# Moving one chunk's scaling to VectorE and its transposes to TensorE in the first stage of a fused attention and feed-forward kernel

## Chip, cores, metric

One core of a Trainium2 chip. The metric is the device time of one execution in microseconds (us). A profile's *span* is some 1.8 us shorter than the time of the same execution, because it starts with the first recorded instruction. "Fast" runs are those at the normal granted clock.

## The reference, cut to what matters

```python
def rmsnorm(x, g):                       # q, k: (8, 12, 448, 64), per head
    rms = np.sqrt(np.mean(x * x, axis=-1, keepdims=True) + 1e-06)
    return x / rms * g
scores = scale * np.matmul(q_n, k_n.transpose(0, 1, 3, 2))
attn = ...                               # softmax of the scores (cut)
x = np.matmul(attn, v)                   # -> (3584, 768)
h = x @ w_in                             # 768 -> 2048
g = h + np.sin(alpha * h) ** 2 / (alpha + 1e-09)
out = g @ w_out                          # 2048 -> 768
```

## The kernel before

It works by batch. Batch b has an *attention stage* (three chunks of four heads; scores, exponentials, values) and a *first product* (h and the sine). The second product of batch b-1 fills TensorE's gaps in the attention stage of batch b. So the first attention stage (b = 0) has no filler but dummy products ("warm"), and the second (b = 1) is the first to be interleaved. Before a chunk's scores it needs square, reduce, rsqrt, scale, and a transposition of q and k. The first three chunks ("early") do the scaling on VectorE and the transposition on TensorE. All later chunks use GpSimd and DMA:

```python
early = ci < NC                                     # NC = 3 chunks a batch
def scale(w):
    eng = nc.vector if early else nc.gpsimd         # inv in PSUM if early, in SBUF if not
def transpose():                                    # DMA
    nc.sync.dma_start_transpose(out=qkT[pi]..., in_=st.n[...])
def pe_transpose(pairs, ws=(0, 1), act=False):      # 28 transposes into one PSUM pair, then copies
    tp = bank_pair("tp", BF16)
```

PSUM is handed out as four pairs of banks. The allocator takes the pair that its own model expects to be free first, and the instruction then waits for the pair's last reader:

```python
def bank_pair(name, dtype=F32):
    slot = min(free_at, key=free_at.get)
    ...
def values(n=1):                                    # the last two value pairs of a batch: n = 2
    if n == 1:
        return attend(pairs.popleft())
    for js in (range(NJ - 1), [NJ - 1]):            # six tiles of one pair, six of the other,
        for pi in list(pairs)[:n]:                  # then the last tile of each
            attend(pi, js)
```

The end of the first stage (S_ is one tile of scores with its warm products, A_ a value pair; cut):

```python
A_(), S_(1), S_(1), S_(1)
c2.pe_transpose((0, 1))
S_(2), A_(), S_(2)
step_of(NC, 3, 4)()                # fourth chunk (NC): reduce
S_(2), S_(1), A_()
step_of(NC, 5, 6)()                # rsqrt, scale on GpSimd, DMA transpose
load_w_out(1)
S_(1), S_(1), A_(), S_()
step_of(NC + 1, 3, 4)()            # fifth chunk: reduce
S_(), A_(2)
```

## Time and profile before

| | before |
|---|---|
| time, median of 3 | 439.43 us |
| span of the profiled execution | 438.3 us (time 440.08 us) |
| first attention stage | 0 to 39.56 us, TensorE idle 5.95 us |
| first product | 39.56 to 57.73 us, no idle |
| second attention stage | 57.73 to 92.72 us, TensorE idle 4.11 us |
| all after it | 345.58 us, idle only in the last output's drain |

A row of the timeline reads: start, length, engine, source line, operation, output<-inputs, shape, count, and in brackets the engine's idle time ahead of it and what ended that. Source lines named here: L294 scores, L297 exponentials, L314 values, L320 and L321 reciprocals, L326 normalization of the values, L246 scaling, L269 TensorE transposes, L276 copies of the transposed tile, L353 first product, L400 second product, L406 output copies.

One view is needed that the prediction does not show: TensorE in the last two value pairs of the first stage.

```profile
35.88 0.38 PE L314 MATMUL av<-expT,vb 64*64 64x448 bf16 x2 [0.23 <-ACT expT L297]
...
37.73 0.38 PE L314 MATMUL av<-expT,vb 64*64 64x448 bf16 x2 [0.71 <-ACT expT L297]
```

Five tiles of the first pair run from 35.88, then TensorE waits 0.71 us for the sixth tile's exponential.

### The profile page before, as it was taken

Reading aid. Unit: us, or ns where it says so; the run is one execution under the profiler, and the core shown is the slowest. Engines: PE = TensorE matmul, PEld = TensorE weight load, DVE = VectorE, ACT = ScalarE, POOL = GpSimd, SP = SyncE. Lnnn points to the kernel's source line nnn. Section 1 sums busy time; section 2 is a strip of 40 time slices with the busy share of each in tenths; the row PEclk is TensorE's granted clock in tenths of the full one; section 3 lists DMA queues with packets and bytes.
Section 4 is the critical chain, followed back from the end, with each engine's and each line's share of the span. In section 5 each row is a group of like instructions: output and inputs, shape, how many; then the busy total and the mean of one; then the engine's idle time right before and its main releaser. Section 6 shows DMA issues by size and latency. Waiting matters only on the chain.

```text
span 438.3 us, 9452 instructions
## 1 busy us (share of the span) xinstructions
PE 423.9 (97%) x3817; PEld 220.3 (50%) x3819; DVE 227.5 (52%) x329; ACT 340.0 (78%) x532; POOL 280.5 (64%) x264
## 2 busy tenths in 40 slices
PE   7889988999999999999999999999999999999996
PEld 3434543555555555555555554555555555555563
DVE  4767463547454574455636574555635474246511
ACT  5888897878888788878888788887878788788600
POOL 4969869917797469937699269956599276003300
PEclk9999999999999999999999999999999999999999
DMA  7999999790067804593076903596063901320022
GB/s 252 210 255 189 188 214 243 226 231 6 20 181 194 176 2 94 152 211 114 2 199 167 204 0 50 167 214 141 2 179 100 125 0 28 90 56 0 1 72 73
DMA packets 70096, 55.09 MB, mean 126 GB/s; under 512 B 41492, under 2 KB 65828, under 8 KB 70052
## 3 DMA queue, kind: packets, MB, share of 16 engines
q1 hardware_dynamic: 56690, 40.97, 36.9%
q0 software_dynamic: 12416, 11.81, 18.0%
q10 hardware_dynamic: 946, 1.70, 1.0%
q8 instruction: 30, 0.49, 0.4%
q14 instruction: 14, 0.11, 0.1%
HBM read 45.62 MB, written 11.01 MB: 129 GB/s over the span
## 4 chain that ended last, share of the span: by engine, by line
PE 83%; ACT 4%; DMA 4%; POOL 4%; DVE 2%; issue 2%; POOLq 0%; ACTq 0%
PE ops L400 31%; PE hps L353 30%; PE av L314 13%; PE sc L294 8%; DMA qkT<-qkn 3%; POOL qk L224 2%; ACT expT L297 2%; ACT s L332 1%; DMA qk<-in_k_dram 1%; POOL sq L221 1%; DVE ms L227 1%; DVE xT L326 1%; ACT s L337 1%; POOL vb L135 1%; DVE qkn L246 0%
## 5 line engine op out<-in xcount | busy, mean ns | idle before, releaser
L297 ACT ACTIVATE expT<-sc 128x896 bf16<-128x896 f32 x168 | 144.5, 912 | 31.9 <-PE sc L294 31.2
L400 PE MATMUL ops<-w_out_sb,g_sb 128*128 128x384 bf16 x896 | 156.7, 327 | 0.0
L353 PE MATMUL hps<-xT,w_in 128*128 128x448 bf16 x768 | 146.7, 353 | 0.0
L335 POOL TENSOR_TENSOR s<-s 128x448 f32<-128x448 f32 x61 | 56.7, 934 | 114.6 <-ACT s L332 100.4
L400 PEld LDWEIGHTS <-g_sb 128*128 128x128 bf16 x896 | 83.1, 98 | 69.5 <-issue 18.4
L340 DVE SCALAR_TENSOR_TENSOR g_sb<-s,inv_alpha_sb,hps 128x448 bf16<-128x448 f32 x128 | 80.8, 676 | 63.3 <-POOL s L335 62.3
L353 PEld LDWEIGHTS <-w_in 128*128 128x128 bf16 x768 | 74.5, 98 | 71.5 <-issue 2.9
L326 DVE TENSOR_TENSOR xT<-av,rec 64x448 bf16<-64x448 f32 x96 | 59.7, 622 | 70.6 <-ACT rec L321 51.5
L332 ACT ACTIVATE s<-hps,alpha_sb 128x448 f32<-128x448 f32 x128 | 74.9, 627 | 26.7 <-PE hps L353 23.9
L246 POOL TENSOR_TENSOR qkn<-qk,inv 128x448 bf16<-128x448 f32 x84 | 76.2, 940 | 10.0 <-POOL qk L224 6.0
L221 POOL TENSOR_TENSOR sq<-qk 128x896 f32<-128x896 f32 x44 | 73.4, 1686 | 0.0
L314 PE MATMUL av<-expT,vb 64*64 64x448 bf16 x672 | 69.2, 349 | 1.8 <-ACT expT L297 0.9
L314 PE MATMUL av<-expT,ones 64*64 64x448 bf16 x672 | 69.2, 349 | 0.0
L294 PE MATMUL sc<-qkT 64*64 64x448 bf16 x672 | 51.8, 361 | 4.4 <-DMA qkT<-qkn 1.8
L227 DVE TENSOR_REDUCE ms<-sq 128x14 f32<-128x896 f32 x44 | 46.8, 1081 | 16.3 <-POOL sq L221 16.1
L406 DVE COPY osb<-ops 128x768 f32<-128x768 f32 (+1 forms) x33 | 27.6, 837 | 46.7 <-PE ops L400 40.1
L224 POOL TENSOR_TENSOR qk<-qk,gg 128x896 f32<-128x896 f32 x24 | 50.2, 2091 | 1.8 <-ACT gg L171 1.7
L314 PEld LDWEIGHTS <-vb 64*64 64x64 bf16 x672 | 37.6, 107 | 14.0 <-issue 2.6
L314 PEld LDWEIGHTS <-ones 64*64 64x64 bf16 x672 | 37.1, 107 | 11.6
L337 ACT ACTIVATE s<-s 128x448 f32<-128x448 f32 x67 | 38.6, 577 | 3.5 <-DVE g_sb L340 0.5
L294 PEld LDWEIGHTS <-qkT 64*64 64x64 bf16 x672 | 15.3, 104 | 34.4 <-issue 28.5
L320 ACT ACTIVATE rec<-av 128x448 f32<-128x448 f32 x48 | 26.1, 544 | 3.7 <-PE av L314 3.2
(44 smaller groups left out, 136.6 us busy)
## 6 DMA issues: line engine op xcount, KB each, us to landing
qk<-in_q_dram SPq DMA_DIRECT2D x24, 448.0 KB, 5.5
qk<-in_k_dram SPq DMA_DIRECT2D x22, 448.0 KB, 5.9
out_dram<-osb SPq DMA_DIRECT2D x39, 192.0 KB, 2.8
vb<-in_v_dram POOLq DMA_DIRECT2D x32, 168.0 KB, 6.6
w_in<-in_moe_w_in_dram POOLq DMA_DIRECT2D x4, 768.0 KB, 11.0
w_out_sb<-in_moe_w_out_dram POOLq DMA_DIRECT2D x2, 1536.0 KB, 25.2
out_dram<-osb SPq DMA_DIRECT2D x26, 96.0 KB, 6.2
qk<-in_k_dram ACTq DMA_DIRECT2D x2, 448.0 KB, 6.0
```

The source lines that it names most:

```text
L221: nc.gpsimd.tensor_mul(st.sq[w], qk[ci][:, w], qk[ci][:, w])
L224: eng.tensor_mul(qk[ci][:, 0], qk[ci][:, 0], gg.to_broadcast([P, 2 * NJ, D]))
L246: eng.tensor_mul(n[:, :, hi, :], x[:, hi], inv[:, hi].unsqueeze(2).to_broadcast([P, NJ, D]))
L294: nc.tensor.matmul(sc[key_rows(pp, hi), pp, :S], qkt[r, 1, j * REST:(j + 1) * REST], qkt[r, 0, :], start=True, stop=True)
L297: nc.scalar.activation(expT[c, j], sc[:, :, :S], ACT.Exp, scale=SCALE)
L314: nc.tensor.matmul(av[o, part, :S], ones[r, :] if part else vb[b][r, hp, j, :], expT[pi // 2, j][r, pi % 2, :], start=(j == 0), stop=(j == ...
L326: nc.vector.tensor_mul(xT[b][r, hp, :], av[r, 0, :S], rec[o, :])
L332: nc.scalar.activation(s1, hps, ACT.Sin, scale=alpha_sb[:, m, :])
L335: nc.gpsimd.tensor_mul(s2, s1, s1)
L340: nc.vector.scalar_tensor_tensor(g_sb[:, m, (b % 2) * S:(b % 2 + 1) * S], s2, inv_alpha_sb[:, m, :], hps, op0=ALU.mult, op1=ALU.add)
L353: nc.tensor.matmul(ps[:, m % 2, :S], w_in_sb[m * 2 // MT][:, kt, m % (MT // 2) * P:(m % (MT // 2) + 1) * P], x[:, kt, :], start=(kt == 0), ...
L400: nc.tensor.matmul(st["ps"][:, k, :HALF], g_sb[:, m, c0:c0 + P], w_out_sb[:, m, half * HALF:(half + 1) * HALF], start=(m == 0), stop=(m == ...
```

## The change

The intent: take the fourth chunk off GpSimd and the DMA queues, which are both behind when the second stage begins, and put it into the first stage, where TensorE runs dummies. With it come several smaller edits. The core of the diff:

```diff
-        give_back(ps, passes(0.2) + 0.5)          # alpha
+        give_back(ps, passes(0.2) + 2.0)
-        early = ci < NC
+        early = ci <= NC
-        def scale(w):
+        def scale(w, heads=(0, 1)):               # may now be cut by heads
-        if m % 2 == 0 and (b or m <= MT // 2):    # squares on GpSimd
+        if m % 2 == 0:
-            for js in (range(NJ - 1), [NJ - 1]):
+            for j in range(NJ):
                 for pi in list(pairs)[:n]:
-                    attend(pi, js)
+                    attend(pi, [j])
@@ first stage
+    spread_alpha()                                # moved here, ahead of the third rsqrt
     c2.rsqrt()
     ...
+    load_w_out(1)                                 # moved ahead
+    c4.fold_g()                                   # moved ahead
     A_(), S_(1), S_(1), S_(1)
     c2.pe_transpose((0, 1))
-    S_(2), A_(), S_(2)
-    step_of(NC, 3, 4)()
-    S_(2), S_(1), A_()
-    step_of(NC, 5, 6)()
-    load_w_out(1)
-    S_(1), S_(1), A_(), S_()
+    S_()
+    c3.reduce(0), c3.reduce(1)
+    A_(), S_(2)
+    c3.rsqrt()
+    S_(2)
+    c3.scale(0), c3.scale(1)
+    load_qk(NC + 3)
+    S_(1), A_(), S_(1), S_(1)
+    c3.pe_transpose((0, 1))
+    A_(), S_()
@@ beside the first product (i: after the i-th pair of tiles)
-    (2, c4.fold_g), (4, c4.scale(0)), (5, c4.scale(1)), (6, transpose)
+    (2, c4.scale(0, [0])), (3, c4.scale(0, [1])), (4, c4.scale(1, [0])), (5, c4.scale(1, [1])),
+    (6, transpose), (6, the sixth chunk's second square)
```

More of the change, by code (lines that the diff above doesn't have):

```diff
@@ L244, in scale @@
             inv = st.inv[w].rearrange("p (hi j) -> p hi j", hi=2)
-            for hi in range(2):
+            for hi in heads:
                 eng.tensor_mul(n[:, :, hi, :], x[:, hi], inv[:, hi].unsqueeze(2).to_broadcast([P, NJ, D]))
-            st.scaled += 1
-            if st.scaled == 2:
+            st.scaled += len(heads)
+            if st.scaled == 4:
                 for ps, time in st.inv_ps:
@@ L452 @@
     c0.pe_transpose((0, 1), (0,))
-    spread_alpha()
     c1.reduce(0), c1.reduce(1)
@@ L499 @@
     begin_norm(NC)
-    step_of(NC, 0, 1, 2)()
+    c3 = norm[NC]
+    c3.square(0), c3.square(1)
+    c3.fold_g()
     nc.gpsimd.tensor_copy(gate, qk[NC + 1][:, 1, 0, 0:1])
@@ L504 @@
     begin_norm(NC + 1)
-    step_of(NC + 1, 0, 1)()
+    c4 = norm[NC + 1]
+    c4.square(0), c4.square(1)
     for part in load_v(1):
         part()
+    load_w_out(1)
+    c4.fold_g()
     A_(), S_(1), S_(1), S_(1)
     c2.pe_transpose((0, 1))
-    S_(2), A_(), S_(2)
-    step_of(NC, 3, 4)()
-    S_(2), S_(1), A_()
-    step_of(NC, 5, 6)()
-    load_w_out(1)
-    S_(1), S_(1), A_(), S_()
-    step_of(NC + 1, 3, 4)()
+    S_()
[8 more added lines that the diff above has]
+    A_(), S_()
+    c4.reduce(0), c4.reduce(1)
     S_(), A_(2)
-    c4 = norm[NC + 1]
     c4.rsqrt()
     beside = beside_h(0)
-    for i, task in ((2, c4.fold_g), (4, lambda: c4.scale(0)), (5, lambda: c4.scale(1)), (6, step_of(NC + 1, 6))):
+    for i, task in ((2, lambda: c4.scale(0, [0])), (3, lambda: c4.scale(0, [1])), (4, lambda: c4.scale(1, [0])),
+                    (5, lambda: c4.scale(1, [1])), (6, step_of(NC + 1, 6)), (6, beside[3].pop())):
         beside.setdefault(i, []).append(task)
```

## The prediction

> **What bounds the kernel now.** I read the page's rows of tenths first, then busy time by stretch (cut where the first product and the third stage begin), then what TensorE waited for, then the order of work from 0 to 95 us. The columns of the first fence are each engine's busy us in the stretch (number of instructions), clock, DMA share and GB/s.
>
> ```profile
> PE   7889988999999999999999999999999999999996
> ...
> PEclk9999999999999999999999999999999999999999
> DMA  7999999790067804593076903596063901320022
> ```
>
> ```profile
> 0.00:39.56 39.56, 33.61 (x390) 15.34 (x392) 24.84 (x42) 29.96 (x48) 29.74 (x37) 1.00 0.94 229
> 39.56:57.73 18.17, 18.17 (x101) 9.40 (x98) 10.75 (x17) 15.25 (x28) 16.71 (x16) 1.00 1.30 185
> 57.73:92.72 34.99, 30.88 (x349) 16.16 (x348) 16.67 (x23) 29.23 (x45) 27.09 (x25) 1.00 1.05 229
> 92.72:438.30 345.58, 341.26 (x2988) 179.43 (x2984) 175.25 (x250) 265.56 (x413) 206.93 (x188) 1.00 0.43 100
> ```
>
> The last stretch is 345.58 us with 341.26 of TensorE work; the missing 4.3 us are the drain of the last output, after TensorE's last product. So from 92.72 us on TensorE never waits, at clock 1.00, and the change edits nothing there (the "b or" of its square test already gave those batches an even split). What can be won lies ahead of 92.72 us: 39.56 - 33.61 = 5.95 us idle in the first attention stage, none in the first product, 34.99 - 30.88 = 4.11 us in the second attention stage. That is 10.06 us, 2.3% of 439.43, before asking how much of it this change reaches. TensorE's waits in the second stage (58 to 95 us: total us, times, longest), and its timeline there:
>
> ```profile
> PE sc L294 <- DMA qkT<-qkn: 1.8, 2, 1.4
> PE sc L294 <- ACT expT L297: 1.0, 1, 1.0
> PE av L314 <- DVE osb L406: 0.9, 1, 0.9
> PE sc L294 <- DVE g_sb L340: 0.3, 1, 0.3
> ```
>
> ```profile
> 63.88 0.38 PE L294 MATMUL sc<-qkT 64*64 64x448 bf16 x4 [1.03 <-ACT expT L297]
> ...
> 70.18 0.38 PE L294 MATMUL sc<-qkT 64*64 64x448 bf16 x2 [0.37 <-DMA qkT<-qkn]
> 71.97 0.76 PE L294 MATMUL sc<-qkT 64*64 64x448 bf16 x10 [1.41 <-DMA qkT<-qkn]
> ```
>
> These four waits are 3.98 us, nearly all of the 4.11. The 1.78 us on the transpose belong to the fifth chunk (index 4), whose DMA transposes come late; the other 2.2 us are ScalarE and VectorE running behind. The timelines of GpSimd, of the SP queue and of ScalarE say why:
>
> ```profile
> 39.13 3.63 POOL L246 TENSOR_TENSOR qkn<-qk,inv 128x448 bf16<-128x448 f32 x4
> 42.71 1.21 POOL L192 DMA_DIRECT2D w_out_sb<-in_moe_w_out_dram  x1
> ...
> 55.19 3.63 POOL L246 TENSOR_TENSOR qkn<-qk,inv 128x448 bf16<-128x448 f32 x4
> ```
>
> ```profile
> 42.78 5.41 SPq L256 DMA_TRANSPOSE qkT<-qkn  x2
> ...
> 58.84 5.48 SPq L256 DMA_TRANSPOSE qkT<-qkn  x2
> ```
>
> ```profile
> 52.73 0.63 ACT L332 ACTIVATE s<-hps,alpha_sb 128x448 f32<-128x448 f32 x1 [0.98 <-POOL s L335]
> ...
> 61.62 1.28 ACT L530 ACT_TABLE_LOAD   x1
> 62.91 0.92 ACT L297 ACTIVATE expT<-sc 128x896 bf16<-128x896 f32 x1
> ```
>
> GpSimd scales the fourth chunk at 39.13, the fifth only at 55.19 to 58.8, and the fifth's two transposes are issued at 58.84 and landed by 71.9. ScalarE waits for GpSimd's squares in the first product, does three more squares itself, and starts its first exponential at 62.91, 5.0 us after the product ended on TensorE (57.9). In the next stage, which has no idle TensorE, that lag is 114.17 - 111.06 = 3.1 us.
>
> **What the Trainium skill says.** "VectorE: DVE Perf Modes", section The three transpose paths: TensorE's path is the faster one but leaves its result in PSUM. The trace agrees on the shape of the cost: 28 transposes take 0.89 us, and VectorE then copies twice (1.16 us). "DMA: Bandwidth & Descriptors", Issuing engines are not separate DMA queues: transfers of all issuers interleave on the same 16 engines. Here a transpose takes 10.9 to 15.2 us to land before 75 us, while weights stream, against a median of 3.4 us over the kernel. "SBUF — State Buffer", in its account of engine and DMA ports: a VectorE operation with two SBUF inputs and a GpSimd one that reads SBUF can exclude each other. The "early" chunks keep one input (inv) in PSUM; the trace shows no stretching, each VectorE multiply 0.61 to 0.62 us while GpSimd squares. So I add nothing for it.
>
> **The change, part by part.**
> (1) *Fourth chunk to VectorE and TensorE.* Removed from GpSimd: 3.63 us at 39.13. Removed from the DMA engines: one pair of transposes; between 46 and 58 us its queue took 34% and 44% of the engines, about 0.39 x 12 = 4.7 us of all 16. Added to VectorE: 2.2 us of multiplies (as for chunk 2 at 23.10) and 1.16 us of copies. Added to TensorE: 0.89 us; two filler products (0.43 us) go.
> In the first stage ScalarE sets the pace: from 28.95 to 38.49 us it never idles (exponentials of 0.83 us a tile, 1.06 us a reciprocal), while TensorE runs filler. So ScalarE's chain decides what the 0.89 us costs. The filler that goes stood at 26.65, just where ScalarE waited 1.04 us for scores: that gives about 0.4 us back. The alpha copy in front of the third rsqrt (0.42 us of VectorE, moved from 12.16 to the gap at 21.6 to 23.1) takes one more PSUM pair, so the first value product may wait for a later exponential: -0.2 us. VectorE gets 3.4 us more into 26.6 to 43.2, where it is busy 11.65 of 16.6 us; I estimate the scaling done at about 33.3, as TensorE arrives for it, costing 0.2 to 0.5 us of stall that ScalarE's queue partly hides.
> (2) *The last two value pairs tile by tile.* Before, TensorE waits 0.71 us at 37.73 for the sixth tile's exponential with the other pair's five tiles in hand. These now fill the wait: -0.6 us. The last exponential still ends about 38.4, and only four matmuls of each pair (0.38 us) can follow it, so the first product starts near 38.8 instead of 39.56. Parts (1) and (2) with alpha: about 0.7 us gained, 0 to 1.2.
> (3) *First product.* Three squares (3 x 0.55 = 1.65 us) move from ScalarE to GpSimd (3 x 0.93 = 2.8 us). GpSimd has lost 3.63 us of scaling, and the fold (2.09) and the weight issue (1.2) go ahead of the product. Per 2.28 us of TensorE work it then has one square and one fifth-chunk multiply, 0.93 + 0.94 = 1.87 us, so it keeps up; ScalarE has two sines and one square, 1.65 us. The product itself stays at 18.2 us.
> ScalarE's lag falls from 5.0 to about 2.5 to 3.1 us: the waits of 1.03 and 0.27 should go, 1.3 us.
> (4) *Fifth chunk.* Its scaling ends right after the sixth pair's square, about 55.5, and its transposes are issued 3 us earlier, into DMA engines that have 4.7 us less to move ahead of it. They should land by about 66; TensorE, 1.3 + 0.7 us ahead of before, wants them at about 68. So 1.78 us go, with 2 us to spare.
> (5) *Knock-on.* The 0.90 us at 82.48 waits for an output copy queued behind a reduction, itself behind a normalization multiply that waited for a late ScalarE reciprocal. With ScalarE on time most of it should go: 0.6 of 0.9.
> *Sum:* 0.7 + 1.3 + 1.78 + 0.6 = 4.4 us. I keep 0.2 back for a new small wait: 439.43 - 4.2 = **435.2 us**, 1.0% faster, inside the 2% band.
>
> **Rivals.** *A: VectorE or PSUM becomes the limit of the first stage.* Inv and the transposed tile hold one of four PSUM pairs from about 30 to 36 us, so scores rotate over two; the reduction, the scaling and the copies stand in order ahead of the normalizations that free the value pairs. For: VectorE would be some 90% busy there. Against: chunk 2 went the same way at 23 to 28 us. If so, the first stage loses 0.5 to 1.5 us instead of winning 0.7: 436 to 437.4. *B: a DMA wait in place of the one removed.* The sixth chunk's rows of q and k are now fetched at about 34 instead of 48.3, among the weights. The first half of w_out landed at 54.3 and is needed at 57; the second landed at 71.3 and was needed at 72.65. For: 0.92 MB come in front. Against: the second half is issued 3.6 us earlier and 4.7 us of transposing go. If B holds: 1 to 2 us back, 436 to 437. *C: the transposes were hidden anyway*, and another releaser turns up at the same matmuls, since ScalarE is close to busy throughout the second stage (29.23 of 34.99 us). Against: the next stage has more TensorE work and no wait at all. It would leave 1 to 1.5 us: about 436.5.
>
> **Range and chances.** The best case takes away all 3.98 us of the second stage and 1.6 us of the first: 433.9. The bad case has A and half of B: 437.4. To be faster by 2% it would have to save 8.8 us of the 10.06 idle, of which some 3 lie in the load before 12 us, which it doesn't touch; to be slower by 2% it would need a new stall in every batch, and nothing there is edited. So 433.8 to 437.4; faster 0.02, same 0.97, slower 0.01.
>
> **What would show it.** Right: the start of the first product near 38.8; first exponential of the second stage within 3.2 us of the product's end; no wait on the DMA transpose there; second-stage idle at most 0.8 us; one pair of DMA transposes fewer (40 for 42), 28 more on TensorE; the tail after the second stage unchanged at about 345.6 us. Wrong: a wait on the scaling ahead of the transposes over 0.6 us, a first product that starts after 39.6, a wait of the output products for w_out, or a tail that changed by more than 0.5 us, which would mean that a later stage was not so indifferent as I read it.

## The result

The changed kernel took 437.75 us (437.36 to 438.06, 4 runs) against 439.37 us before (4 runs). The ratio of the fast runs is 0.9961, 95% interval 0.9944 to 0.9978. A ratio here is worked out by the measuring program from the fast runs of both kernels in the same rounds, so it is not quite the ratio of the medians. The change is faster by 0.4%, inside the 2% band, but by 1.6 us and not by the 4.2 us forecast; 437.75 lies above the range's upper end of 437.4.

**Clock note.** Executions differ in the mean granted TensorE clock, 0.99 to 1.00. Over all rounds before's spans at a clock of 0.997 or more run from 436.1 to 438.3 us (39 runs, mean 437.2), and the changed kernel's from 435.4 to 435.7 (6 runs, mean 435.6). With a lower clock they are 437.4 to 437.9 (10 runs) and 436.3 to 437.8 (4 runs).

The profile after, by stretch, cut at the same events as before (engine busy us, clock, DMA share, GB/s):

```profile
0.00:41.14 41.14, 33.41 (x415) 16.08 (x418) 28.98 (x48) 29.99 (x48) 31.88 (x38) 1.00 0.95 234
41.14:59.31 18.17, 18.17 (x100) 9.40 (x97) 11.36 (x18) 15.68 (x28) 12.62 (x14) 1.00 1.28 216
59.31:90.50 31.19, 29.98 (x350) 15.85 (x348) 15.35 (x21) 27.22 (x41) 28.14 (x25) 1.00 0.92 184
90.50:435.70 345.20, 341.25 (x2988) 179.42 (x2984) 175.26 (x250) 265.42 (x413) 206.73 (x188) 1.00 0.44 102
```

The second stage shrank as forecast, from 34.99 to 31.19 us (forecast 31.31). The product stayed at 18.17, the rest at 345.2. The first stage grew from 39.56 to 41.14 instead of shrinking to 38.9. TensorE's waits in the second stage (its part of the list of waits), and its row at the first score tile of the fifth chunk, which waited 0.37 and 1.41 us before and now waits for nothing:

```profile
PE av L314 <- DVE osb L406: 0.9, 1, 0.9
PE sc L294 <- ACT expT L297: 0.3, 1, 0.3
```

```profile
69.74 0.76 PE L294 MATMUL sc<-qkT 64*64 64x448 bf16 x12
```

The transposes of the fifth chunk on the SP queue of the changed kernel; then the summary of the DMA transposes that it issued between 40 and 63 us, which are this pair; then the same summary of before, which holds the fourth chunk's pair, since no landing is on record there for the fifth's:

```profile
57.62 3.83 SPq L256 DMA_TRANSPOSE qkT<-qkn  x2
```

```profile
DMA to landing us min/median/max: 7.2/7.5/7.8
```

```profile
DMA to landing us min/median/max: 10.9/13.1/15.2
```

They are issued 16.5 us after the product's start, as forecast (16.7), and land 7 to 8 us later, ahead of need.

Now the end of the first stage, TensorE and then ScalarE:

```profile
34.13 0.89 PE L269 MATMUL tp<-ident,qkn 64*128 64x64 bf16 x28
...
36.68 0.38 PE L314 MATMUL av<-expT,ones 64*64 64x448 bf16 x2
36.72 0.35 PE L314 MATMUL av<-expT,vb 64*64 64x448 bf16 x2
38.55 0.38 PE L314 MATMUL av<-expT,vb 64*64 64x448 bf16 x2 [1.49 <-ACT expT L297]
38.56 0.56 PE L314 MATMUL av<-expT,ones 64*64 64x448 bf16 x4
...
41.14 0.55 PE L353 MATMUL hps<-xT,w_in 128*128 128x448 bf16 x2
```

```profile
36.55 0.54 ACT L320 ACTIVATE rec<-av 128x448 f32<-128x448 f32 x1 [0.81 <-PE av L314]
37.12 0.58 ACT L321 ACTIVATE rec<-rec 128x448 f32<-128x448 f32 x1
37.60 1.71 ACT L297 ACTIVATE expT<-sc 128x896 bf16<-128x896 f32 x2
41.08 0.54 ACT L320 ACTIVATE rec<-av 128x448 f32<-128x448 f32 x1 [1.77 <-PE av L314]
```

Two things are new. ScalarE, which from 28.95 us to its last exponential at 38.49 never waited before, waits 0.81 us for a value pair that stands behind the 28 transposes. (A wait of 0.36 us for the value pair before it, at 32.97, is new too; it stays when the transposes are moved away, see e14.) And of the last two value pairs only four matmuls, one tile, run at 36.68; then TensorE waits 1.49 us, until the first of ScalarE's last two exponentials has ended, and all the other tiles come after it.

### The profile page after: what moved, and what is told of

Its sections match the earlier page's. It is cut to its first block, busy times and chain, and to the rows that moved or that the text cites. A ratio compares the mean times of both kernels' runs of the same rounds, so it can differ in the third digit from the quotient of the medians.

```text
span 435.7 us, 9509 instructions
## 1 busy us (share of the span) xinstructions
PE 422.8 (97%) x3843; PEld 220.8 (51%) x3845; DVE 230.9 (53%) x335; ACT 338.3 (78%) x529; POOL 279.4 (64%) x263
## 4 chain that ended last, share of the span: by engine, by line
PE 81%; ACT 2%; DVE 2%; issue 0%
PE ops L400 32%; PE hps L353 29%; PE av L314 13%; PE sc L294 7%; ACT expT L297 2%; DVE ms L227 1%; DVE osb L406 0%; DVE g_sb L340 0%; DVE xT L326 0%; ACT rec L321 0%; ACT inv L236 0%; ACT inv L237 0%; ACT rec L320 0%
## 5 line engine op out<-in xcount | busy, mean ns | idle before, releaser
L335 POOL TENSOR_TENSOR s<-s 128x448 f32<-128x448 f32 x64 | 59.4, 932 | 116.6 <-ACT s L332 103.1
L246 POOL TENSOR_TENSOR qkn<-qk,inv 128x448 bf16<-128x448 f32 x80 | 72.6, 937 | 7.5 <-POOL qk L224 7.0
L294 PE MATMUL sc<-qkT 64*64 64x448 bf16 x672 | 50.9, 361 | 1.8 <-DVE qkT L276 1.4
L337 ACT ACTIVATE s<-s 128x448 f32<-128x448 f32 x64 | 36.9, 577 | 2.8
```

Source lines behind the costliest of these rows:

```text
L246: eng.tensor_mul(n[:, :, hi, :], x[:, hi], inv[:, hi].unsqueeze(2).to_broadcast([P, NJ, D]))
L294: nc.tensor.matmul(sc[key_rows(pp, hi), pp, :S], qkt[r, 1, j * REST:(j + 1) * REST], qkt[r, 0, :], start=True, stop=True)
L335: nc.gpsimd.tensor_mul(s2, s1, s1)
```

## The experiments

18 runs, in five groups; runs of a group share a chip and the runs of the kernel before. Each was correct.

### How far one trace of before stands for the others

Five traces of the same code, unedited: e1, and later three (e13, e17, e18), beside the one above; and a second trace of the changed kernel (e2).

> The kernel before, unchanged, to see how far one trace of it stands for the others. Theory 1 (the one profiled execution of before was an average one): the first product starts at 39.56 us again, the second stage again waits some 1.8 us for the fifth chunk's transposes, span about 438. Theory 2 (that execution was slow by 0.6 us, as its 440.08 us against a median of 439.4 suggests): the second stage's idle time differs by 0.5 us or more, in the wait on the DMA transpose. Time: ratio 1.000.

> The changed kernel, unchanged, for the same reason. Time ratio to before 0.996. The first product starts at 41.1 us, with one wait of 1.5 us in the last two value pairs, and the second stage has about 1.2 us idle. If instead the late start at 41.1 was an accident of one execution, it moves by 0.5 us or more here.

> The kernel before once more, for its trace alone. If the wait on the fifth chunk's transposes is a matter of chance from one execution to the next, an execution at full clock shows anything from 0 to 1.8 us of it, and its span is 436.3 plus that wait; the theory that the profiled 1.78 us was at the upper end expects 0 to 1.2 us here. Rival (1.78 us is the usual size): 1.5 us or more.

> The kernel before, for its trace alone: as e13. A wait on the fifth chunk's transposes of 0 to 1.2 us at full clock if the profiled 1.78 us was at the upper end of what chance gives; 1.5 us or more if it is the usual size.

> The kernel before, for its trace alone: as e13 and e17. Span equals about 436.3 us plus the wait on the transposes, where the clock is full.

| trace | clock in stage 1 | product starts | first score tile to product | wait on the fifth chunk's transposes | stage 2 lasts | stage 2 ends | span |
|---|---|---|---|---|---|---|---|
| before | 1.00 | 39.56 | 27.56 | 1.78 | 34.99 | 92.72 | 438.3 |
| before, e18 | 1.00 | 39.51 | 27.55 | 1.11 | 34.30 | 91.98 | 437.6 |
| before, e13 | 1.00 | 40.69 | 27.63 | 0.49 | 33.71 | 92.57 | 438.2 |
| before, e1 | 0.96 | 41.18 | 29.18 | 0 | 32.79 | 92.14 | 437.7 |
| before, e17 | 0.96 | 41.23 | 29.18 | 0 | 32.76 | 92.16 | 437.7 |
| changed | 1.00 | 41.14 | 28.92 | 0 | 31.19 | 90.50 | 435.7 |
| changed, e2 | 1.00 | 40.82 | 28.92 | 0 | 31.19 | 90.18 | 435.4 |

The fourth column counts from TensorE's first score tile, which itself starts between 11.7 and 13.1 us from one execution to the next. Counted so, the first stage repeats within 0.1 us at full clock, and differences between kernels are read from it below. The tile in before and in the changed kernel:

```profile
12.00 0.86 PE L294 MATMUL sc<-qkT 64*64 64x448 bf16 x8 [0.16 <-DVE qkT L276]
```

```profile
12.22 0.86 PE L294 MATMUL sc<-qkT 64*64 64x448 bf16 x8 [0.48 <-DVE qkT L276]
```

e1's time was 439.04 us, ratio 0.9991 (0.9979 to 1.0003); e2's 437.39 us, ratio 0.9969 (0.9952 to 0.9985); the single looks took 440.01, 439.51 and 439.41 us. The wait is indeed 0 to 1.8 us. It depends on how late TensorE is: in these five traces of before the second stage ends between 91.98 and 92.72 whether the first stage ended at 39.5 or at 41.2. So in them a first stage that is up to 1.7 us longer cost nothing, since the transposes then were ready on time. (All five spans lie above the mean of 437.2; what the shorter executions, down to 436.1, look like is not known.) In the changed kernel the second stage takes 31.19 us in both traces, and a late start goes straight through. Its own late start is not what removed the wait: in e15 below, with the product at 39.99, 0.7 us earlier than in e13, there is none either.

Late starts have two visible reasons. In e1 the granted clock falls to 0.50 for some 3.4 us in the first stage, and the value products there take 0.58 us instead of 0.35. Timeline and stretch 25 to 30 us of e1, then the same products in the first trace of before:

```profile
28.07 0.58 PE L314 MATMUL av<-expT,ones 64*64 64x448 bf16 x2
```

```profile
25.00:30.00 5.00, 4.80 (x67) 2.36 (x66) 2.70 (x5) 2.51 (x3) 1.86 (x3) 0.69 1.08 287
```

```profile
28.15 0.35 PE L314 MATMUL av<-expT,ones 64*64 64x448 bf16 x2
```

The other reason lies at the very start. In e13 (and in e12 below) the 15 dummy products ahead of the first transposes take 5.17 us (5.16) instead of before's 3.41, although the clock column reads 1.00, and the first score tile comes at 13.1 us instead of 12.0.

My expectation for e13, e17 and e18 that a span is 436.3 us plus the wait did not hold for e13, whose stage 1 was 1.1 us late at full clock.

### The order of the last two value pairs

e3 gives the changed kernel the old order; e4 gives the kernel before the new one.

```diff
# e3_after_old_order, against the changed kernel (e4 is the reverse edit on before)
-            for j in range(NJ):
+            for js in (range(NJ - 1), [NJ - 1]):
                 for pi in list(pairs)[:n]:
-                    attend(pi, [j])
+                    attend(pi, js)
```

> The changed kernel with the last two value pairs in the order of before (six tiles of one pair, six of the other, then the last of each). Theory A (the tile-by-tile order is what costs: the second of the two pairs gets the PSUM pair that the exponential of the last tile but one still reads, so its first product blocks TensorE for 1.5 us, while five tiles of the first pair that are ready stand behind it): the wait of 1.5 us turns into one of about 0.8 us later on, the first product starts at 40.2 to 40.4 instead of 41.1, and the time falls by 0.7 to 0.9 us. Rival B (the transposes on TensorE and ScalarE's delay after them are all of it): the start stays at 41.0 or later and the time is that of the changed kernel.

> The kernel before with only the tile-by-tile order of the last two value pairs taken over. My prediction's step: the second pair's tiles fill the wait of 0.71 us, the first product starts about 0.6 us earlier (38.9), time down by 0.6 us. Theory A: the second pair's PSUM pair is free only when the exponential of the last tile but one has been computed (about 37.7), so TensorE waits from about 36.1 to 37.7 with 13 of 14 tiles still to do; the first product starts at 40.1 to 40.3, 0.6 us later than before, and the time rises by 0.6 us.

e3: 436.50 us, ratio 0.9943 (0.9931 to 0.9955), 0.9 us under e2 of the same group (at full clock 436.35 to 436.53, but for one run of 438.03, against 437.14 to 437.40). The product starts at 40.19 (40.82 in e2), and the wait is 0.73 us:

```profile
38.36 0.38 PE L314 MATMUL av<-expT,vb 64*64 64x448 bf16 x2 [0.73 <-ACT expT L297]
...
40.19 1.12 PE L353 MATMUL hps<-xT,w_in 128*128 128x448 bf16 x5
```

e4: 439.48 us, ratio 1.0002 (0.9987 to 1.0016), not clear of noise against before. Its trace is clear. It and e1 had the same dip of the clock, and where e1 waits 0.71 us in the last two pairs and starts the product at 41.18, e4 waits 1.46 and starts at 41.66:

```profile
39.08 0.38 PE L314 MATMUL av<-expT,vb 64*64 64x448 bf16 x2 [1.46 <-ACT expT L297]
```

Counted from the first score tile, the tile-by-tile order costs 0.75 us in either kernel: 28.92 us (changed) against 28.17 (e3), and 29.93 (e4) against 29.18 (e1). In before that is not seen in the time, as a late first stage was seen to cost nothing there.

The second pair's inputs are not what is missing: both pairs of a chunk read the same exponentials (`expT[pi // 2, j]` in the kernel's `attend`), and the first pair's tile has just run with them. What is missing is the output. By the allocator's own arithmetic, worked through from the code, the second of the two value pairs gets the PSUM pair that held the last score tile but one, in both kernels. Its first matmul can't start until that tile's exponential has read it. In the old order it comes after six tiles of the first pair; in the new one it is the second tile in TensorE's queue, with twelve behind it. That the wait ends at the exponential is shown by the traces; that it is this PSUM pair follows from the code, and e3 and e4 go as it says.

### What the transposes on TensorE cost

e7 takes three dummy products away ahead of them, e8 puts them behind the fourth value pair, e14 moves them into the first product. All have the old order of values.

```diff
# e7_old_order_nofill
-    S_(1), A_(), S_(1), S_(1)
+    S_(), A_(), S_(), S_()
     c3.pe_transpose((0, 1))
# e8_old_order_tp_later
-    c3.pe_transpose((0, 1))
-    A_(), S_()
+    A_()
+    c3.pe_transpose((0, 1))
+    S_()
# e14_tp_in_product: the call removed from the first stage, and beside the first product
+    (4, lambda: c3.pe_transpose((0, 1)))
```

> The changed kernel with the value pairs' order of before and, on top, without the three single filler products ahead of the fourth chunk's transposes. Theory (in the first stage ScalarE sets the pace, and it waits 0.8 us for the fourth value pair because 0.89 us of transposes stand in front of it): 0.4 us of filler less ahead of the transposes lets that value pair end 0.4 us sooner, ScalarE's wait falls to about 0.4 us, the first product starts at about 39.8 instead of 40.2, time down 0.4 us against the old order alone (ratio to before about 0.9935). Rival (the scaling on VectorE is the limit, ends at 33.6 us, and TensorE would only wait there): no change. Second rival: fewer fillers bring the clock down, and the time rises.

> The changed kernel with the value pairs' order of before and the fourth chunk's transposes after the fourth value pair instead of ahead of it. ScalarE's wait for that pair should vanish (0.8 to 0.1 us or less) and its last exponential end 0.7 us earlier. If ScalarE's chain alone sets the end of the first stage, the first product starts at about 39.5. If PSUM does (the fifth value pair gets the PSUM pair of the transposed tile and waits for VectorE's two copies, until about 37.6 us, with 14 tiles of 0.19 us to follow), it starts at 40.2 to 40.4, and nothing is won.

> The changed kernel with the value pairs' order of before, and the fourth chunk's 28 transposes put into the first product, where TensorE never waits, instead of the first stage. Theory (in the first stage they cost as much as they last, since ScalarE then waits 0.8 us for the value pair behind them; there was no slack for them): the first stage ends 0.7 to 0.9 us earlier (start of the product at about 39.4), the product grows by about 0.9 us, time equal within 0.2 us to the old order alone. Rival (the first stage hides them and something else makes it long): the first stage ends as before, the time rises by 0.9 us.

e7: 436.64 us, ratio 0.9951 (0.9933 to 0.9969). From the first score tile to the product it takes 28.17 us, as in the two traces of the old order alone (e3, e15): nothing won. The 0.4 us come back as a wait of 0.35 for the scaling and of 0.43 for VectorE's normalization, as the first rival said: VectorE is level with ScalarE here.

e8: 438.91 us, ratio 0.9998 (0.9983 to 1.0013), product start 42.11, worse than I expected of either branch (29.88 us from the first score tile, 1.7 more). The next value pair takes the transposed tile's PSUM pair and waits for VectorE's copies of it:

```profile
39.33 0.38 PE L314 MATMUL av<-expT,vb 64*64 64x448 bf16 x2 [2.47 <-DVE qkT L276]
```

e14: 436.53 us, ratio 0.9943 (0.9928 to 0.9958). The product starts at 39.33 (old order alone 40.19 and 39.99). Counted from the first score tile that is 27.25 us against 28.17, so 0.92 less, and the product lasts 19.10 instead of 18.17 us. ScalarE's wait of 0.81 us is gone:

```profile
35.49 0.55 ACT L320 ACTIVATE rec<-av 128x448 f32<-128x448 f32 x1
```

Its full-clock spans, 434.6 to 434.9, are those of the old order (434.6 to 434.8 but for one run). So the transposes cost what they last, about 0.9 us, in either place: the first stage had no slack for them.

### Which part removed the wait on the fifth chunk's transposes

e5 sends the fourth chunk through GpSimd and DMA again within the changed kernel. e9 gives the kernel before only the fifth chunk's part; e10 takes that part out of the changed kernel.

```diff
# e5_after_chunk3_dma
-        early = ci <= NC
+        early = ci < NC
-    c3.pe_transpose((0, 1))
+    c3.transpose()
# e10_after_c4_late (e9_before_c4_early: the reverse edit on before)
-    c4.fold_g()                                   # ahead of the first product
-    (2, c4.scale(0, [0])), (3, c4.scale(0, [1])), (4, c4.scale(1, [0])), (5, c4.scale(1, [1])), (6, ...)
+    (2, c4.fold_g), (4, c4.scale(0)), (5, c4.scale(1)), (6, transpose)
```

> The changed kernel with the fourth chunk scaled on GpSimd and transposed by DMA again, all else of the change kept. Theory (taking one pair of transposes off the DMA engines is what removes the wait on the fifth chunk's transposes; on TensorE and ScalarE the 28 transposes cost about 0.6 us of the first stage): the first product starts some 0.6 us earlier than in the changed kernel (about 40.2), and the second stage waits 1 to 4 us for DMA transposes, the fourth chunk's included, since they are issued at about 46 now; time 0.5 to 2.5 us above the changed kernel. Rival (the earlier scaling on GpSimd and the earlier weights are what removes it): the second stage has no DMA wait, and the time is equal or 0.6 us below the changed kernel.

> The kernel before with only the fifth chunk's part of the change: its gain folded in ahead of the first product, its scaling cut by heads and spread over the product, one square of the sixth chunk after it; the fourth chunk stays on GpSimd and DMA. Theory (the wait on the fifth chunk's transposes goes only if the fourth chunk's pair is off the DMA engines): its transposes are issued at about 57 to 58 but land at 69 or later, the second stage still waits 0 to 1.5 us for them in some executions, spans of full clock scatter over 436.5 to 438 as before's, ratio 0.998 to 1.000. Rival (issuing them earlier is enough): no DMA wait, spans within 0.5 us of each other near 436.5, ratio 0.997 or less.

> The changed kernel with the fifth chunk's fold, scaling and the square placed as in the kernel before: the complement. Theory (the fourth chunk's transposes off the DMA engines free them, whatever the issue time): the fifth chunk's transposes are issued at about 61 and land within about 8 us, by 69.5, as TensorE needs them; the second stage waits at most 0.5 us for them, time within 0.5 us of the changed kernel's. Rival (the issue time is what counts): wait of 1 us or more on them, time up by 1 us or more.

e5: 444.26 us, ratio 1.0122 (1.0104 to 1.0139), slower than I thought. The fourth chunk's transposes, now issued at 46.22, are what TensorE waits for, 4.6 us. It is some 7 us above the changed kernel, and not all of that is the wait: right after it the granted clock is 0.50 from 66 to 69 us. It shows what the fourth chunk costs there, but its late issue mixes with the load on the DMA engines:

```profile
65.46 0.62 PE L294 MATMUL sc<-qkT 64*64 64x448 bf16 x6 [4.56 <-DMA qkT<-qkn]
```

e9: 438.89 us, ratio 1.0011 (0.9988 to 1.0034); full-clock spans 436.4 to 437.9, where before's of the same group were 436.1 to 438.0. In its trace, one with the clock dip, the transposes are issued at 56.94 and the second stage, 31.53 us, has no wait on them; e1 and e17, also dipped, have none either and last 32.8. So in the trace it gains 1.2 us and in time nothing. I have no full-clock trace of it; that the wait is there in those runs fits their scatter but is not shown.

e10: 440.47 us, ratio 1.0032 (1.0013 to 1.0052). There is no wait on a DMA transpose, as the first theory said, and yet the second stage takes 35.04 us, which neither expected. GpSimd, with eight squares now, finishes the last two at 62.8, and the score tile that needs their PSUM pair waits:

```profile
61.02 1.82 POOL L335 TENSOR_TENSOR s<-s 128x448 f32<-128x448 f32 x2
```

```profile
63.30 0.38 PE L294 MATMUL sc<-qkT 64*64 64x448 bf16 x4 [2.12 <-DVE g_sb L340]
```

The fold ahead of the product and the scaling cut in four are thus not there for the transposes alone. They are what lets GpSimd take the extra squares.

Which part removed the wait on the fifth chunk's transposes therefore stays open. e5 mixes two effects, e9 was traced only in an execution late enough to have no such wait in before either, and in e10 the wait of 2.12 us ahead of it makes TensorE late again.

### Squares, alpha, and the wait that stayed

```diff
# e6_after_sq_on_act
-        if m % 2 == 0:
+        if m % 2 == 0 and (b or m <= MT // 2):
# e12_after_alpha_early: spread_alpha() back behind the first chunk's transposes
# e11_old_order_reduce_late, e15 (old order alone), e16 (as e11): in the second stage
-    (14, step_of(n4, 3)), (15, step_of(n4, 4)), ... (18, step_of(n4, 5))
+    (19 if b == 1 else 14, step_of(n4, 3)), (19 if b == 1 else 15, step_of(n4, 4)), ... (20 if b == 1 else 18, step_of(n4, 5))
```

> The changed kernel with the last three even squares of the first batch on ScalarE again. Theory (ScalarE's lag behind the first product was set by its own squares): the first exponential of the second stage comes 4.2 to 4.8 us after the product's end instead of 3.6, TensorE waits about 1 us for an exponential in the second stage, time up by 0.5 to 1.0 us. Rival (ScalarE was held back by GpSimd's backlog alone, which the rest of the change cleared): lag and waits stay, time equal within 0.2 us.

> The changed kernel with the spread of alpha back at its old place. Theory (alpha's extra PSUM pair makes the first value pair wait 0.2 us for an exponential, as predicted, and the rest of the first stage soaks it up): the 0.23 us wait at 21.5 to 21.8 goes, the start of the first product moves by less than 0.3 us, time within 0.2 us of the changed kernel. Rival (the move helps, since it frees VectorE at 12 us for the reductions of the second chunk): product start later by 0.3 us or more.

> The changed kernel with the value pairs' order of before, and in the second stage the two reductions of the eighth chunk behind the output copy instead of ahead of it, on VectorE. That copy frees the PSUM pair for which the next value pair waits 0.9 us in every trace so far, of before too. If the queue order on VectorE is the cause, the copy starts when its last product ends, the wait falls to about 0.5 us and the time by 0.4 us (ratio near 0.993). If ScalarE's lateness is (as I had predicted), nothing changes.

> The changed kernel with the value pairs' order of before, again, beside the next run on the same chip: ratio to before 0.994 to 0.996, product start near 40.2.

> The same with the two reductions behind the output copy in the second stage, again: the wait of a value pair for that copy is 0.2 instead of 0.9 us, and the time lies 0.5 to 0.7 us under the run before it in this list, on the same chip. If the first comparison across two chips had misled, they are equal.

e6: 437.59 us, ratio 0.9965 (0.9951 to 0.9979), that of the changed kernel. First exponential 3.9 us after the first matmul of the second product (3.3 in e2, 5.2 in before by the same measure), second stage 31.48 against 31.19 us. The squares are worth 0.3 us at most; the rest of ScalarE's lag fits GpSimd's backlog: in e10, where GpSimd is behind again, the same measure is 5.6 us.

e12: 437.25 us, ratio 0.9973 (0.9956 to 0.9990). The wait of 0.23 us is gone; the first stage from the first score tile of the second chunk to the product is 21.76 us long instead of 22.05. The move costs 0.3 us there, but wins as much ahead of it: from the first score tile of all to that of the second chunk it is 6.87 us in the changed kernel and 7.17 in e12. Over the whole stretch the two have 28.92 and 28.93 us, and in time it does not show either (full-clock spans 435.4 to 435.5 but for two of 436.5 and 436.6, of which the profiled one started late, against 435.4 to 435.7).

e11: 436.03 us, ratio 0.9943 (0.9926 to 0.9959). The wait of a value pair for an output copy, 0.9 us in every trace with the reductions ahead of the copy, is 0.2. VectorE in e3 and then in e11:

```profile
76.19 2.08 DVE L227 TENSOR_REDUCE ms<-sq 128x14 f32<-128x896 f32 x2
78.30 0.96 DVE L406 COPY osb<-ops 128x768 f32<-128x768 f32 x1
```

```profile
77.79 0.96 DVE L406 COPY osb<-ops 128x768 f32<-128x768 f32 x1 [1.47 <-PE ops L400]
78.66 2.07 DVE L227 TENSOR_REDUCE ms<-sq 128x14 f32<-128x896 f32 x2
```

The copy was queued behind a reduction; it starts when its product ends now. The second stage falls from 31.19 to 30.53 us (e16: 30.52). On one chip, e15 took 437.11 us (ratio 0.9955, 0.9940 to 0.9969) and e16 436.95 us (0.9950, 0.9934 to 0.9966). The 0.7 us are in the traces; in the times they are not clear of noise, since four of e15's five runs had the clock dip and two of e16's six, and two more of e16's spans are 1.3 us longer than its shortest, for a reason that was not traced (a late start as in e12 would fit). The best version measured is thus the changed kernel with the old order of values, with or without the later reduction, and with the transposes in either place: 0.994 to 0.996 of before and faster than the changed kernel, by 0.9 us where both were on one chip (e2, e3).

## Why the prediction was wrong

- **Part (2), "These now fill the wait: -0.6 us": this step failed.** The order cost 0.75 us in the first stage instead (e3, e4), and 0.9 in the changed kernel's time. I asked when the tiles' exponentials were ready and not whether the second pair had its PSUM by then.
- **Part (1), the transposes: mis-sized.** For them I allowed 0.2 to 0.5 us of stall until the scaling is done, partly hidden. There is no wait on the scaling in the changed kernel; they cost 0.92 us (e14), about what they last. I had read ScalarE's unbroken row as TensorE having room. But ScalarE waits for the value pair behind the transposes, so TensorE, ScalarE and VectorE were level. The rest of part (1), 0.4 us from the filler less 0.2 for alpha, was about right as a sum: e14, with the old order and without the transposes in the stage, has 27.25 us against before's 27.56. Alpha's 0.2 did not cost anything net (e12).
- Together, the first stage from the first score tile on became 1.36 us longer (28.92 against 27.56) instead of 0.7 shorter. Of these 2.06 us part (2) is 1.35 and the transposes about 0.8; the rest went 0.1 better. The product starts at 40.82 to 41.14 instead of 38.86, 2.0 to 2.3 us of the 2.55 us by which 437.75 exceeds 435.2. A longer first stage was my rival A, with 436 to 437.4, but for other reasons (scores over two PSUM pairs, VectorE's queue); the order of the value pairs was not in it. Of my own signs of being wrong, the product's start after 39.6 came true.
- **Second stage: right in size, partly by luck.** 34.99 to 31.19 us against 31.31 forecast, with no wait on the transposes, as forecast; which of parts (1) and (4) took it away is open. The waits of 1.03 and 0.27 us on ScalarE and VectorE gave 1.0 of 1.3 us. The knock-on of part (5), 0.6 us off the wait for the output copy, failed: it was not ScalarE's lateness but the queue order on VectorE (e11). What made up for it was not foreseen: TensorE's time in the score products fell from 7.13 to 6.28 us for the same 84 matmuls, which are less spread out. The idle time left is 1.21 us, not at most 0.8.
- **The base.** The trace I summed from belonged to an execution of 440.08 us, and I took the sum off the median of 439.43. Its wait of 1.78 us was the largest of five traces (0, 0, 0.49, 1.11, 1.78), and its span of 438.3 equals the longest of the 39 at full clock. That is 0.65 us of the miss; the 0.2 us kept back, a second stage 0.1 us better and a tail 0.4 us shorter go the other way.
- **Rival B and the tail: as read.** No wait for w_out appeared, and the stretch after the second stage is 345.2 us, within the 0.5 us allowed. TensorE's work in it is unchanged (341.25 us); the drain of the last output is what is 0.4 us shorter, which was not looked into.

## What to carry to other kernels

When independent work is interleaved to fill a wait, ask of every piece where its output buffer comes from. Here one tile whose buffer was still being read held up TensorE, and with it twelve tiles queued behind. A wait on a transfer that lands at about the same time whatever the engine does is no sum that a change simply takes off: look at it in several executions (0 to 1.8 us here). And when single traces are compared, count from an event that comes after the scatter of the start: by the product's start e14 wins 0.66 or 0.86 us over the old order alone, depending on the trace, and counted from the first score tile 0.92 over either. Lastly, this stage, with several engines level, had no free place for 0.9 us of work, although one of them ran dummy products there.

## What the Trainium skill lacked or had wrong

- "TensorE: Matmul & The Clock Gate", HAM oscillation, gives one figure for keeping the clock up: no idle gaps of TensorE above about 3.4 us. e5 agrees: after its wait of 4.56 us the clock was 0.50 from 66 to 69 us. But the figure does not cover e1, where the clock fell (0.69 mean over 25 to 30 us, products at 0.58 instead of 0.35 us) after waits of only 1.07 and 0.20 us, with 28 transposes (0.89 us) between them. The same page's Part 4 says that transposes do not count as busy in the same way, which would fit; no run here separates the two, and the first trace of before has the same transposes and nearly the same waits (1.07 and 0.21 us) and no fall. Of 49 timed executions of before 10 had a mean clock under 0.997; where in them the clock fell is seen in the traces of e1 and e17 only, in this place in both.
- "DMA: Bandwidth & Descriptors", DMA Transpose (X-bar), gives no time for a transpose that shares the engines with other transfers. Here the fourth chunk's pair landed in 10.9 and 15.2 us while weights streamed (before), the fifth's in 7.2 and 7.8 us with the weights nearly in (changed kernel, whose last weight load landed 26.3 us after its issue at 38.5), and the median over the kernel before was 3.4 us.
- "Perfetto Trace Analysis", Optimization Strategy, says to find the gaps and what ends them. No page warns that a gap of one trace may be absent in the next: this one was 0 to 1.8 us in five traces of the same code.
